# Two token chunks through one pass over the weights in the first MLP of an attention and two-MLP kernel

## The chip, the cores and the metric

One core of one Trainium2 chip runs the whole program. The metric is device time in microseconds of one execution, the median of several runs; lower is better. A profiled execution of the kernel before gives the rows that are quoted.

## The reference

Attention over 2 batches, 8 heads, 1152 keys and head size 64, with queries averaged in pairs (576 per head), then two MLPs of 1152 tokens, model width 512 and hidden width 2048. Everything is float32. The weights `w_in`, `w_out` of both MLPs reach the chip as 64-bit words, which the kernel turns into float32 itself.

```python
q_pool = q.reshape(B, H, S // factor, factor, D).mean(axis=3)
scores = scale * np.matmul(q_pool, k.transpose(0, 1, 3, 2))
attn = np.exp(scores - np.max(scores, axis=-1, keepdims=True))
attn = attn / (np.sum(attn, axis=-1, keepdims=True) + 1e-09)
x = (attn @ v)                      # then to 1152 tokens x 512
...
h = x @ w_in                        # first MLP
g = np.where(h > 0.0, h, alpha * (np.exp(np.minimum(h, 0.0)) - 1.0))
x = g @ w_out
...
h = x @ w_in                        # second MLP
sp = np.where(h > 20.0, h, np.log1p(np.exp(np.minimum(h, 20.0))))
out = (h * np.tanh(sp)) @ w_out
```

## The kernel before

**Numbers in two parts.** Each operand of a product is kept as a rounded part (`h`, written with a cast to F32R on ScalarE, ACT) and the remainder (`l`, a subtraction on VectorE, DVE, or GpSimd, POOL). A product is three matmuls: high by high, high by low, low by high. PE is TensorE, SP the engine whose queue issues all DMAs.

**Attention.** `Attention.run` (line 696) writes a list of events for 72 tiles of 128 queries: scores (`wide`, `rest`), their maxima on DVE, exponentials on ACT, turning the probabilities with PE (`pst`), splitting them into two parts on ACT, DVE and POOL, and the product with the values (`psv`). Every event has a due time in `PP['x']`, in units of tiles; the list is sorted by it, and that is the order of every engine's queue. The last events (`finish`, line 684) multiply by the reciprocal sums and write `xh` and `xl`, the tokens in two parts, 576 per batch; `xl` is line 694.

**Weights.** There are 32 tiles of weights in each MLP: 16 steps over the hidden width, each with one tile of `w_in` and one of `w_out`, 128x512. In `need` their number is j = 2 * step + (0 for `w_in`, 1 for `w_out`). A tile is converted from 64-bit words by a chain of one Abs on ACT and four operations on DVE (`Weights.chain`, lines 821 to 826, in the attention; `weight`, lines 1040 to 1051, in the MLPs), then cast and subtracted (lines 1064 and 1067; `PP['wd']` lists the tiles whose subtraction is on DVE, the others are on POOL). Five tiles are converted in the attention and stay in SBUF (`fs`, `gs`). Twelve more (`cs0` to `cs11`, `PP['ncs']`; those not in `PP['d1']`) are converted in the attention, stored to DRAM and loaded again in the MLP, since SBUF has no room for them. The tiles in `d1` are converted in the first MLP. While the first MLP runs, many tiles of the second are converted and stored too (`PP['c2']`), and each tile of the second MLP then takes the place of one of the first.

**MLPs.** Each MLP goes through three chunks of tokens (`z1`: 512, 384 and 256 columns; `z2`: three of 384), and each chunk through all 16 steps, so there are 96 steps in a row. A step s has `U{s}` (`up`, line 946: twelve matmuls into one PSUM tile), the gate `g{s}_0` and on (`gate`, line 986), `D{s}` and `E{s}` (`down`, line 958: the eight matmuls with the gate's high part, and four with the low part, summed over the 16 steps in PSUM). PSUM has eight banks: a ring of four for `up` and four for the sums. The gate of the first MLP reads and writes the PSUM tile itself: Relu and Exp on ACT, one operation on DVE (line 1001), the cast to `gh` on ACT (1025), the subtraction to `gl` on DVE (1027). At the end of a chunk `evac` writes the sums to SBUF. `PP['y']` has a due time for each of these events and each link of a weight's chain, in steps; they are sorted, and that is again the order of every queue. On PE it begins like this:

```
U0 U1 U2 U3 D0 U4 E0 D1 E1 U5 D2 E2 U6 U7 D3 U8 E3 D4 E4 D5 U9 E5 U10 D6 D7 E6 U11
```

Of the kernel before, what the change touches and what calls it, by code (L numbers as in the profile page):

```python
# [24 lines left out]
P = 128  # L25
# [18 lines left out]
    'd1': [1, 4, 7, 10, 12, 13, 15, 17, 18, 20, 21, 23, 24, 26, 27, 29, 30, 31],  # L44
    'c2': {'1': 15, '3': 13, '5': 18, '7': 19, '9': 20, '11': 25, '13': 22, '15': 21, '17': 24, '19': 24, '21': 26, '23': 27, '25': 28, '27': 29, '29': 29, '31': 31, '30': 17, '0': 30, '24': 30, '18': 7, '12': 6, '16': 11, '22': 17},
    'ng': 4,
    'wd': [1, 4, 2, 0, 42, 15, 43, 11, 26, 57, 37, 21, 56, 28, 31, 38, 47, 46, 61, 45, 60, 17, 30, 18, 22, 6],
    'upb': 4,
    'man': 'pavgs',
    'wa': [5, 7, 8, 9, 10, 11, 12, 13],  # L50
# [8 lines left out]
    'z1': [512, 384, 256],  # L59
    'z2': [384, 384, 384],  # L60
    'pool': [0, 2, 4, 5, 8, 10, 11, 14, 15, 17, 20, 22, 23],
    'ncs': 12,
# [794 lines left out]
def build(ctx, tc, q, k, v, w1_in, w1_out, w2_in, w2_out, out):  # L857
# [55 lines left out]
    with ExitStack() as actx:  # L913
# [7 lines left out]
        Attention(nc, tc, actx, q, k, v, ident, xh, xl, ps2, ps1, raw).run(aside)  # L921

    wa, wp, gp, tmp = pool("wa", 1), pool("wp", 1), pool("gp", 1), pool("mtmp", PP.get('tb', 2))
    ups, accs = pool("ups", PP['upb'], space=PSUM), pool("accs", 8 - PP['upb'], space=PSUM)
    for key in need:
        if key == PP['odd']:
            W.place[key] = [spare.pop(), wp.tile([P, DM], F32R, name="wo")]
# [225 lines left out]
```

## Time and profile before

| what | us |
|---|---|
| median of 3 runs | 683.97 |
| lowest and highest | 683.75, 684.83 |
| the profiled execution | 684.13 |
| its span, first to last instruction | 682.4 |

The profile has 11870 instructions. In its rows a line like L954 is a line of the kernel; `out<-in` are the names of tiles; a busy time is the sum over a group, and a mean is of one instruction. Matmuls overlap, so the mean of one is longer than the time from one to the next, and the ends of matmuls are modelled.

### The profile page before, as it was taken

Reading aid. Unit: us, or ns where it says so; the run is one execution under the profiler, and the core shown is the slowest. Engines: PE = TensorE matmul, PEld = TensorE weight load, DVE = VectorE, ACT = ScalarE, POOL = GpSimd, SP = SyncE. Lnnn points to the kernel's source line nnn. Section 1 sums busy time; section 2 is a strip of 40 time slices with the busy share of each in tenths; the row PEclk is TensorE's granted clock in tenths of the full one; section 3 lists DMA queues with packets and bytes.
Section 4 is the critical chain, followed back from the end, with each engine's and each line's share of the span. In section 5 each row is a group of like instructions: output and inputs, shape, how many; then the busy total and the mean of one; then the engine's idle time right before and its main releaser. Section 6 shows DMA issues by size and latency. Waiting matters only on the chain.

```text
span 682.4 us, 11870 instructions
## 1 busy us (share of the span) xinstructions
PE 666.1 (98%) x4007; PEld 602.2 (88%) x4007; DVE 586.2 (86%) x1111; ACT 480.2 (70%) x1125; POOL 266.8 (39%) x308
## 2 busy tenths in 40 slices
PE   7999999999999998999999999999999999999997
PEld 5898989888888887888888999999999999989996
DVE  5999899999898998789998887787998886977885
ACT  5999999999999999576765553576655543535453
POOL 2778787878787888352220000133230100000000
PEclk9999999999999999999999999999999999999999
DMA  7678586848675651665443676647120000101001
GB/s 218 160 180 232 134 219 161 216 103 191 184 173 147 170 161 32 197 228 182 167 140 138 214 225 194 201 125 227 51 79 1 1 0 1 48 0 47 0 1 48
DMA packets 65181, 88.64 MB, mean 130 GB/s; under 512 B 22296, under 2 KB 40544, under 8 KB 65120
## 3 DMA queue, kind: packets, MB, share of 16 engines
q1 hardware_dynamic: 65120, 87.88, 45.4%
q8 instruction: 32, 0.52, 0.3%
q14 instruction: 29, 0.24, 0.1%
HBM read 59.24 MB, written 11.57 MB: 104 GB/s over the span
## 4 chain that ended last, share of the span: by engine, by line
PE 80%; ACT 12%; DVE 3%; issue 2%; DMA 1%; POOL 1%; SPq 0%; ACTq 0%; DVEq 0%; POOLq 0%
PE up L954 29%; PE acc L984 29%; PE psv L667 7%; PE pst L627 7%; PE wide L572 5%; ACT a L596 4%; ACT whole L642 2%; ACT th L652 2%; PE rest L572 2%; ACT a L594 1%; DMA qr<-in_q_dram 1%; DVE neg L582 1%; ACT avlo L680 1%; ACT kh L485 1%; DVE tl L654 1%
## 5 line engine op out<-in xcount | busy, mean ns | idle before, releaser
L954 PE MATMUL up<-xh,wp 128*128 128x384 f32 (+2 forms) x576 | 154.0, 336 | 0.0
L434 POOL TENSOR_TENSOR tl<-whole,th 128x384 fp32r<-128x384 f32 (+1 forms) x112 | 114.1, 1019 | 9.3
L627 PE MATMUL pst<-ident,a 128*128 128x128 f32 x648 | 103.6, 277 | 7.5 <-ACT whole L642 3.4
L954 PEld LDWEIGHTS up<-xh,wp 128*128 128x128 f32 x576 | 103.6, 188 | 5.3 <-DVE gl L1027 0.4
L954 PE MATMUL up<-xl,wp 128*128 128x384 f32 (+2 forms) x288 | 96.6, 335 | 0.0
L627 PEld LDWEIGHTS pst<-ident,a 128*128 128x128 f32 x648 | 75.2, 140 | 22.4 <-ACT whole L642 8.9
L1067 POOL TENSOR_TENSOR wp<-wt,wp 128x512 fp32r<-128x512 f32 x32 | 45.7, 1441 | 120.8 <-ACT wp L1064 90.6
L667 PE MATMUL psv<-th,vs 128*128 128x320 f32 (+1 forms) x288 | 89.0, 327 | 1.4 <-ACT whole L642 1.0
L667 PE MATMUL psv<-tl,vs 128*128 128x320 f32 (+1 forms) x288 | 79.9, 295 | 0.0
L582 DVE TENSOR_REDUCE neg<-wide 128x1 f32<-128x898 f32 x72 | 78.0, 1083 | 0.4
L433 POOL TENSOR_SCALAR th<-whole 128x384 fp32r<-128x384 f32 (+1 forms) x112 | 61.8, 551 | 39.0 <-ACT whole L642 29.4
L596 ACT ACTIVATE a<-wide,neg 128x896 f32<-128x896 f32 x72 | 73.9, 1026 | 0.8 <-DVE neg L582 0.4
L654 DVE TENSOR_TENSOR tl<-pst,th 128x384 fp32r<-128x384 f32 (+1 forms) x128 | 60.4, 498 | 12.0 <-ACT th L652 11.0
L1004 ACT ACTIVATE e<-up 128x384 f32<-128x384 f32 x48 | 23.7, 494 | 59.2 <-PE up L954 40.5
L984 PE MATMUL acc<-wp,gh 128*128 128x512 f32 x252 | 64.1, 391 | 0.0
L1027 DVE TENSOR_TENSOR gl<-up,gh 128x384 fp32r<-128x384 f32 (+2 forms) x96 | 52.6, 552 | 13.2 <-ACT gh L1025 6.7
L984 PE MATMUL acc<-gh,wp 128*128 128x512 f32 (+2 forms) x336 | 63.8, 335 | 0.0
L1025 ACT CAST gh<-up 128x384 fp32r<-128x384 f32 (+2 forms) x96 | 45.0, 478 | 23.3 <-DVE up L1023 13.6
L984 PEld LDWEIGHTS acc<-gh,wp 128*128 128x128 f32 x336 | 54.8, 189 | 4.4
L652 ACT CAST th<-pst 128x384 fp32r<-128x384 f32 (+1 forms) x128 | 53.3, 455 | 7.5 <-PE pst L627 3.8
L572 PE MATMUL wide<-ks,qh 128*128 128x448 f32 (+1 forms) x160 | 57.7, 375 | 0.0
L667 PEld LDWEIGHTS psv<-th,vs 128*128 128x128 f32 x288 | 54.4, 189 | 3.6 <-ACT whole L642 1.6
(150 smaller groups left out, 1570.4 us busy)
## 6 DMA issues: line engine op xcount, KB each, us to landing
raw<-in_moe_w_out_dram SPq DMA_DIRECT2D x23, 512.0 KB, 4.8
w<-wt SPq DMA_DIRECT2D x35, 256.0 KB, 3.5
wt<-w SPq DMA_DIRECT2D x35, 256.0 KB, 3.2
raw<-in_moe_w_in_dram SPq DMA_DIRECT2D x17, 512.0 KB, 4.9
wp<-in_moe_w_in_dram SPq DMA_DIRECT2D x13, 512.0 KB, 6.9
kr<-in_k_dram SPq DMA_DIRECT2D x16, 288.0 KB, 5.3
vr<-in_v_dram SPq DMA_DIRECT2D x8, 576.0 KB, 4.0
wp<-in_moe_w_out_dram SPq DMA_DIRECT2D x9, 512.0 KB, 6.1
```

The costliest lines, as they stand in the source:

```text
L433: nc.gpsimd.tensor_scalar(hi, x, 1.0, 1.0, op0=ALU.mult, op1=ALU.mult)
L434: nc.gpsimd.tensor_tensor(lo, x, hi.bitcast(F32), op=ALU.subtract)
L572: nc.tensor.matmul(dst, w[:], x[:, cols], start=(o == 0), stop=(o == len(ops) - 1))
L582: nc.vector.tensor_reduce(neg[:], wide[:, :, :WW + 1], axis=AX.XY, op=ALU.max, negate=True)
L596: nc.scalar.activation(a[:, :2 * WW].rearrange("p (c x) -> p c x", c=2), wide[:, :, :WW], AF.Exp, bias=neg[:], accum_out=self.sums[n][:, t ...
L627: nc.tensor.transpose(ps[:, i * P:(i + 1) * P], a[:, j * P:(j + 1) * P], self.ident[:])
L652: nc.scalar.copy(h, src[:, :, x0:x0 + w])
L654: nc.vector.tensor_tensor(l, src[:, :, x0:x0 + w], h.bitcast(F32), op=ALU.subtract)
L667: nc.tensor.matmul(ps[:, :w], self.VS[n % 2][:, h, j].rearrange("p a d -> p (a d)"), t[:, j, :w], start=(c == 1), stop=(c == 2 * NKT))
L954: nc.tensor.matmul(ps, w, x, start=(o == 0), stop=(o == len(ops) - 1))
L984: nc.tensor.matmul(ps[:, :x.shape[1]], a, x, start=(i == 0 and o == 0 and not low), stop=(i == NFF - 1 and low == 1))
L1027: tt(gl, h, gh.bitcast(F32), op=ALU.subtract)
```

## The change

The first two chunks of the first MLP, 512 and 256 tokens, go through the 16 steps together. The new list of steps has three wide steps first, then alternates wide and narrow ones, and ends with three narrow ones; the third chunk (384) and the second MLP follow as before. There are 96 steps still. Each narrow step runs three pairs behind the wide step with the same weights.

Since two chunks are summed at once, PSUM is divided anew: four banks for the wide sums, two for the ring of `up` (tag `up`), and two (tag `upb`) that serve as part of the ring for the first four steps, then hold the four narrow sums, two of 256 columns in each bank, and return to the ring from step 36 on. A gate of the first MLP now begins with a copy of the PSUM tile to SBUF on ACT (`p`), which frees the tile; the four operations that follow read and write `p`.

The number of tiles stored in the attention falls from twelve to nine (`ncs`; `d1` has three more tiles). `wd` loses ten tiles of the first MLP, whose subtractions go to POOL. `wa` (which pool a weight tile's place is taken from) has other tiles. All due times in `x` and `y` are new. On PE the new order is, from the start and around step 13:

```
U0 U1 U2 U3 D0 U4 E0 D1 U5 E1 U6 D2 E2 U7 U8 D3 D4 E3 U9 D5 U10 E4 D6 D7 E5 U11 D8 E6 E7
U12 D9 D10 D11 U13 U14 E8 E9 U15 D12 E10 E11 U16 E12 D13 U17
```

```diff
-    'd1': [1, 4, 7, 10, 12, 13, 15, 17, 18, 20, 21, 23, 24, 26, 27, 29, 30, 31],
+    'd1': [1, 4, 7, 9, 10, 11, 13, 14, 15, 17, 18, 19, 21, 22, 23, 25, 26, 27, 29, 30, 31],
...
-    'wd': [1, 4, 2, 0, 42, 15, 43, 11, 26, 57, 37, 21, 56, 28, 31, 38, 47, 46, 61, 45, 60, 17, 30, 18, 22, 6],
+    'wd': [1, 4, 2, 0, 42, 43, 57, 37, 56, 38, 47, 46, 61, 45, 60, 6],
...
-    'wa': [5, 7, 8, 9, 10, 11, 12, 13],
+    'wa': [5, 7, 9, 10, 11, 13, 14, 15],
...
-    'z1': [512, 384, 256],
+    'z1': [512, 256, 384],
...
-    'ncs': 12,
+    'ncs': 9,
...
-    ups, accs = pool("ups", PP['upb'], space=PSUM), pool("accs", 8 - PP['upb'], space=PSUM)
+    ups, accs = pool("ups", 2, space=PSUM), pool("accs", 4, space=PSUM)
...
-    steps = [(m, c, i) for m in range(2) for c in range(len(Z[m])) for i in range(NFF)]
+    wide, thin = ([(0, c, i) for i in range(NFF)] for c in range(2))
+    lag = 3
+    steps = wide[:lag] + [x for p in zip(wide[lag:], thin) for x in p] + thin[-lag:]
+    steps += [(0, 2, i) for i in range(NFF)] + [(1, c, i) for c in range(3) for i in range(NFF)]
+    paired = 2 * NFF
...
-        hid[s] = ps = ups.tile([P, 512], F32, name="up")[:, :z]
+        hid[s] = ps = ups.tile([P, 512], F32, name="up" if 4 <= s < paired + 4 or s % 2 else "upb")[:, :z]
...
-            acc[m, c] = [accs.tile([P, 512], F32, name="acc") for _ in range(units)]
+            if (m, c) == (0, 1):
+                halves = [ups.tile([P, 512], F32, name="upb") for _ in range(2)]
+                acc[m, c] = [x[:, y:y + 256] for x in halves for y in (0, 256)]
+            else:
+                acc[m, c] = [accs.tile([P, 512], F32, name="acc") for _ in range(units)]
...
-            nc.tensor.matmul(ps[:, :x.shape[1]], a, x, start=(i == 0 and o == 0 and not low), stop=(i == NFF - 1 and low == 1))
+            shared = (m, c) == (0, 1)
+            nc.tensor.matmul(ps[:, :x.shape[1]], a, x, start=(i == 0 and o == 0 and not low and not (shared and u % 2)),
+                             stop=(i == NFF - 1 and low == 1), skip_group_check=shared)
...
         if m == 0:
+            p = t("p")
             if k == 0:
-                act(t("e"), h, AF.Relu, scale=-1.0)
+                nc.scalar.copy(p, h)
             if k == 1:
+                act(t("e"), p, AF.Relu, scale=-1.0)
+            if k == 2:
                 act(t("e"), t("e"), AF.Exp, scale=-1.0)
-            if k == 2:
-                stt(out=h, in0=t("e"), scalar=-1.0, in1=h, op0=ALU.add, op1=ALU.max)
+            if k == 3:
+                stt(out=p, in0=t("e"), scalar=-1.0, in1=p, op0=ALU.add, op1=ALU.max)
+            h = p
```

## Rows read from the trace of the kernel before

**Rows 1.** The page, busy us of each engine, share of the span, instructions.

```profile
PE 666.1 (98%) x4007; PEld 602.2 (88%) x4007; DVE 586.2 (86%) x1111; ACT 480.2 (70%) x1125; POOL 266.8 (39%) x308
```

**Rows 2.** By stage: stretch, length, busy us of each engine (x), PEclk, DMA share, GB/s.

```profile
0.00:20.00 20.00, 15.26 (x88) 10.37 (x89) 12.76 (x23) 12.73 (x30) 7.57 (x21) 1.00 0.79 216
20.00:260.00 240.00, 234.64 (x1653) 212.01 (x1653) 220.43 (x393) 228.93 (x591) 192.35 (x234) 1.00 0.67 170
260.00:278.60 18.60, 16.16 (x110) 13.90 (x109) 15.97 (x33) 15.87 (x39) 11.72 (x16) 1.00 0.10 30
278.60:356.20 77.60, 77.60 (x343) 63.66 (x342) 72.16 (x124) 51.16 (x93) 25.05 (x17) 1.00 0.60 201
356.20:411.00 54.80, 54.80 (x303) 52.98 (x302) 46.03 (x90) 31.10 (x63) 1.30 (x1) 1.00 0.57 183
411.00:460.00 49.00, 49.00 (x355) 49.00 (x354) 37.43 (x78) 27.59 (x67) 8.55 (x7) 1.00 0.58 178
```

**Rows 3.** The page, the chain that ended last, share of the span by engine.

```profile
PE 80%; ACT 12%; DVE 3%; issue 2%; DMA 1%; POOL 1%; SPq 0%; ACTq 0%; DVEq 0%; POOLq 0%
```

**Rows 4.** Shapes on ACT, 20 to 260 us: count, busy, mean ns, idle before.

```profile
L821 ACT ACTIVATE wt<-raw 128x512 f32<-128x512 f32 x12 | 8.3, 691 | 0.0
```

**Rows 5.** Shapes on DVE, 20 to 260 us.

```profile
L826 DVE SCALAR_TENSOR_TENSOR wt<-raw,wt 128x512 int32<-128x512 int32 x12 | 9.9, 824 | 0.0
L824 DVE SCALAR_TENSOR_TENSOR wt<-raw,wt 128x512 int32<-128x512 int32 x13 | 9.5, 728 | 0.0
L823 DVE TENSOR_SCALAR wt<-wt 128x512 int32<-128x512 int32 x13 | 9.1, 698 | 0.0
...
L822 DVE TENSOR_SCALAR wt<-wt 128x512 f32<-128x512 f32 x13 | 6.8, 520 | 0.2
```

**Rows 6.** Timeline of PE, 278.5 to 292 us: start, us, what.

```profile
278.62 0.39 PE L954 MATMUL up<-xh,wf 128*128 128x512 f32 x1
...
289.57 1.98 PE L984 MATMUL acc<-gh,vr 128*128 128x512 f32 x8
```

**Rows 7.** Timeline of PE, 425 to 437 us, a narrow up.

```profile
432.98 0.28 PE L954 MATMUL up<-xh,kr 128*128 128x256 f32 x1
...
434.41 0.86 PE L984 MATMUL acc<-gl,wp 128*128 128x384 f32 x4
```

**Rows 8.** Timeline of ACT, 264 to 292 us, the cast of gate 0.

```profile
286.77 0.58 ACT L1025 CAST gh<-up 128x512 fp32r<-128x512 f32 x1
```

**Rows 9.** Timeline of DVE, 283 to 293 us.

```profile
286.40 1.13 DVE L694 TENSOR_TENSOR xl<-xf,xh 128x576 fp32r<-128x576 f32 x1 [2.02 <-ACT xh L692]
...
288.66 1.64 DVE L1049 SCALAR_TENSOR_TENSOR wt<-wp,wt 128x512 int32<-128x512 int32 x1
```

**Rows 10.** Shapes on ACT, 278.6 to 356.2 us and 411 to 460 us.

```profile
L997 ACT ACTIVATE e<-up 128x512 f32<-128x512 f32 x16 | 9.4, 594 | 2.7 <-PE up L954 2.7
...
L997 ACT ACTIVATE e<-up 128x256 f32<-128x256 f32 x12 | 4.6, 386 | 2.6 <-PE up L954 1.5 <-DVE up L1001 0.7 <-ACT wt L1040 0.4
```

**Rows 11.** Shapes on DVE, 278.6 to 356.2 us.

```profile
L1049 DVE SCALAR_TENSOR_TENSOR wt<-wp,wt 128x512 int32<-128x512 int32 x15 | 13.9, 926 | 0.1
L1051 DVE SCALAR_TENSOR_TENSOR wt<-wp,wt 128x512 int32<-128x512 int32 x15 | 12.9, 859 | 0.2
...
L1001 DVE SCALAR_TENSOR_TENSOR up<-e,up 128x512 f32<-128x512 f32 x14 | 9.4, 686 | 0.1
...
L1067 DVE TENSOR_TENSOR wp<-wt,wp 128x512 fp32r<-128x512 f32 x9 | 6.1, 683 | 0.0
...
L1049 DVE SCALAR_TENSOR_TENSOR wt<-raw,wt 128x512 int32<-128x512 int32 x4 | 2.7, 679 | 0.0
```

**Rows 12.** Waits of ACT, 278.6 to 411 us: total, times, longest us.

```profile
ACT wp L1064 <- DVE wt L1051: 9.1, 6, 2.5
...
ACT wt L1040 <- DVE wt L1049: 4.9, 1, 4.9
```

**Rows 13.** Timeline of POOL, 284 to 300 us.

```profile
288.46 1.29 POOL L1067 TENSOR_TENSOR wo<-wt,qr 128x512 fp32r<-128x512 f32 x1 [1.53 <-ACT qr L1064]
```

More of the change, by code (lines that the diff above doesn't have):

```diff
@@ L992, in t @@
             if (s, x) not in tmps:
-                tmps[s, x] = tmp.tile([P, ZM if x == "e" else max(PP['z2'])], F32, name=x)[:, :h.shape[1]]
+                tmps[s, x] = tmp.tile([P, max(PP['z2']) if x == "n" else ZM], F32, name=x)[:, :h.shape[1]]
             return tmps[s, x]
         if m == 0:
+            p = t("p")
             if k == 0:
-                act(t("e"), h, AF.Relu, scale=-1.0)
+                nc.scalar.copy(p, h)
             if k == 1:
+                act(t("e"), p, AF.Relu, scale=-1.0)
+            if k == 2:
                 act(t("e"), t("e"), AF.Exp, scale=-1.0)
-            if k == 2:
-                stt(out=h, in0=t("e"), scalar=-1.0, in1=h, op0=ALU.add, op1=ALU.max)
+            if k == 3:
+                stt(out=p, in0=t("e"), scalar=-1.0, in1=p, op0=ALU.add, op1=ALU.max)
+            h = p
         else:
@@ L1023, in gate @@
                 stt(out=h, in0=t("p"), scalar=-1.0, in1=h, op0=ALU.mult, op1=ALU.mult)
-        if k == (9 if m else 3):
+        if k == (9 if m else 4):
             nc.scalar.copy(gh, h)
-        if k == (10 if m else 4):
+        if k == (10 if m else 5):
             tt(gl, h, gh.bitcast(F32), op=ALU.subtract)
@@ L1096, in build @@
         add(f'E{s}', down, s, 1)
-        for k in range(11 if m else 5):
+        for k in range(11 if m else 6):
             add(f'g{s}_{k}', gate, s, k)
```

522 rows, old and new, of the table PP are left out of this document.

## The prediction

> **What bounds it now.** I read the page's busy shares first, then a table by stage, then the chain's shares, then the shapes and timelines of the two stages that the change touches. PE is busy 98% of the span [rows 1], so the first guess is that no time is left. The table corrects that in two ways [rows 2]. From 278.6 to 460 us, the first MLP, PE's busy time equals the length of every stretch at full granted clock: 77.60 of 77.60, 54.80 of 54.80, 49.00 of 49.00. Nothing that another engine does faster there can shorten it; it can only be lengthened. From 20 to 260 us, the attention, three engines are nearly full at once: PE 234.64 of 240 us, ACT 228.93 (95.4%), DVE 220.43 (91.8%). PE's figure there is soft, since matmul ends are modelled. Of the chain ACT holds 12% and DVE 3% [rows 3], and with PE full in the MLP these shares belong almost wholly to the attention. So the attention is paced by ACT and PE handing work to each other, with DVE close behind, and it is the one place where removed work can pay.
>
> **The change part by part.** *Nine tiles stored, not twelve.* For each of the three chains removed from the attention ACT does one Abs of 0.691 us [rows 4] and DVE four operations of 0.520, 0.698, 0.728 and 0.824 us, together 2.77 us [rows 5]. Three chains are 2.07 us of ACT and 8.31 us of DVE; three loads and three stores leave SP's queue too, where nothing on the chain waits behind them. What the span gains lies between two ends. Weighted by the chain, ACT's 12% and DVE's 3% of 682.4 us are 82 and 20 us; held against the 278.6 us up to the MLP that is 29% and 7%, so 0.6 + 0.6 = 1.2 us. If DVE's whole relief reached the end it would be 8.3 us. If ACT keeps its idle share, its 2.07 us alone are 2.07 / 0.954 = 2.2 us. I take ACT's 2.2 us, ACT being the fullest engine after PE, and add DVE's chain-weighted 0.6: a gain of 2.8 us.
>
> *Orders anew in the attention.* Nothing else is added or removed there; which instruction stands ahead of which changes throughout. The trace cannot price this. Its room is PE's idle time at both ends: 4.74 us in the first 20 us and 2.44 us from 260 to 278.6 [rows 2]. I take 0 and keep 2 us either way.
>
> *The first steps of the MLP.* The old order has U0 to U3 (10.95 us of matmuls) ahead of D0 [rows 6], and so has the new one. Gate 0's cast ended at 286.77 + 0.58, 2.2 us before D0 [rows 8]; the added copy takes 0.59 us of that, and 1.6 us stay. The new U4 is the first narrow step and reads tokens 512 to 767, whose last part, xl of the last pair, ended at 287.53 [rows 9], 4 us before D0's end at 291.55, behind which U4 stands. Cost 0; with that cover gone, each microsecond of lateness is a microsecond of span.
>
> *One pass for two chunks.* The matmuls are the same in number and width (512, 256 and 384 columns in place of 512, 384 and 256), so PE's own work stays. Twelve take 2.74 us at 512 columns (10.95 / 4) [rows 6] and 1.43 at 256 (434.41 less 432.98) [rows 7]. A pair of steps is 24 matmuls of each width, 5.5 + 2.9 = 8.3 us for two weight tiles, where the old first chunk left 5.5. Weights are due later, but PE did not wait for them: gain 0.
>
> *Copies to SBUF.* ACT gets 48. The nearest rows are its first reads of the same PSUM tiles: 0.594 us at 512 columns and 0.386 at 256 [rows 10], halfway 0.49 at 384; 16 times 1.47 is 23.5 us. ACT is idle for 26.4 + 23.7 + 21.4 = 71.5 us between 278.6 and 460 [rows 2], which hides them.
>
> *Work brought into the MLP.* Three more chains, again 8.3 us of DVE and 2.1 of ACT at most. Ten subtractions of the first MLP go from DVE (0.683 us) [rows 11] to POOL (1.29) [rows 13]: DVE loses 6.8 us, POOL gains 13. DVE, idle for 25.8 us from 278.6 to 460, ends about where it was, and POOL is nearly idle after 356 [rows 2]. Three full loads replace three reloads; the DMA share was 0.60 at most. Cost 0, but see the rivals.
>
> *Ring of first products.* Four PSUM tiles become two while the narrow chunk's sums hold the other two banks. Adding up the new order with the step times above, the time from the end of a U to the U that reuses its tile is mostly 5 to 8 us, in seven cases under 5, the least 2.8 (U13 to U15: U14, E8 and E9 lie between). A copy of 0.59 us fits if ACT is not more than 2.2 us late; its single waits for conversions were 2.5 us long, once 4.9 [rows 12]. Bounds: 0, or seven cases of about 0.7 us, 5 us. I take 0, the nearest row being a PE without any wait in this stage.
>
> **Sum.** The profiled execution's 684.13 us (span 682.4 and 1.7 around it) less 2.8 is 681.3. It lies 0.16 us over the median of 683.97; I forecast medians: 683.97 - 2.8 = 681.2 us.
>
> **The rivals.** *The port (slower).* The copy gives both DVE operations of a first-MLP gate two SBUF inputs where they had one. Such an operation stretches when it meets POOL: the conversion at 288.66 took 1.64 us [rows 9] beside a POOL subtraction from 288.46 to 289.75 [rows 13]. From 278.6 to 356.2 the conversions took 0.926 and 0.859 us on some tiles and 0.679 on others, while the gates, with one input in PSUM, took 0.686 [rows 11]. Worked out from these: about 0.2 us for each of 64 gate operations in the paired pass, 13 us, on a DVE that was busy for 118.2 of the 132.4 us from 278.6 to 411 [rows 2]. With 8.3 us of chains, and less 3.4 us for half of the subtractions, DVE would need 136 us in 132. It decides from the point at which a gate ends later than its D is due; with half of the 13 us, 6.5, reaching PE the time is 681.2 + 6.5 = 687.7 us. Against it: in the first 77.6 us DVE was 93% busy already, and PE did not wait. Chance 0.13. The Trainium skill, SBUF — State Buffer, section "Who interferes with whom", has a rule for this: a VectorE instruction with two SBUF inputs and a GpSimd instruction that reads SBUF exclude each other for a whole instruction. By that rule, with which the 1.64 us agree, the price above is the change's own.
>
> *The ring (slower).* Copies stand in ACT's queue behind its waits for loads and conversions: 681.2 + 5 = 686.2 us, chance 0.07. *Nothing arrives.* The freed time in the attention is taken up by another wait, because PE, ACT and DVE hand the chain around: the chain-weighted 1.2 us or less, 682.8 us or a little over; chance 0.18. *DVE is the true pace.* Then 8.3 us go: 675.7 us. For it: DVE at 92%, with operations stretched there as well (0.824 us, where 0.679 is the undisturbed time); against it, DVE's small part of the chain. Chance 0.10. That the chains are not removed can be excluded: the lists say which tiles are converted early.
>
> **How the numbers follow.** The forecast, chance 0.52, spans 679 to 682.6. A measurement of this kernel can tell about 0.2% (1.4 us) from no change, so faster means below 682.6: 0.52 + 0.10 = 0.62. Same is the third rival, 0.18. Slower is the port and the ring, 0.20. The range runs from 676.5, most of the way to the DVE rival, to 687.5, close to the port's price; about a tenth lies beyond each end.
>
> **What would show it.** Right: the first up matmul starts near 275.8 instead of 278.62; three Abs fewer in the attention (12 stood from 20 to 260 us); ACT still above 95% there and DVE near 90%; PE busy for the whole of every MLP stretch; 48 copies of about 0.59, 0.49 and 0.39 us on ACT. The port: gate operations of more than 0.75 us at 512 columns, and PE idle ahead of acc matmuls, released by DVE or ACT. The ring: PE idle ahead of up matmuls, released by ACT's copy. I am wrong in the main step if the first up matmul does not move, or if PE loses more than 1 us between it and 660 us.

## The result, and the profile after

The changed kernel takes 690.45 us (median of 4 runs, 690.09 to 691.96) where the kernel before took 684.40 beside it (683.75 to 685.22). The ratio is 1.010, interval 1.0088 to 1.0111: slower, by 6.05 us. 681.2 us and faster had been forecast; the range ended at 687.5.

Two numbers split the result. The first up matmul starts at 274.60 us in place of 278.62 [rows 6], so the attention is 4.0 us shorter. From there to the end of the span it takes 690.2 - 274.6 = 415.6 us, before 682.4 - 278.6 = 403.8: the MLPs are 11.8 us longer. The profiled execution took 691.96 us, 1.5 over the median, so that these two numbers add up to 7.8 and not to 6.05; what is read from the profile below belongs to that execution.

The page of the changed kernel: the span, the busy line, and the chain that ended last.

```profile
span 690.2 us, 11927 instructions
...
PE 666.9 (97%) x4007; PEld 605.1 (88%) x4007; DVE 591.8 (86%) x1101; ACT 501.0 (73%) x1173; POOL 289.6 (42%) x318
...
PE 71%; ACT 9%; issue 6%; DVE 5%; DMA 5%; POOL 3%; SPq 0%; POOLq 0%; ACTq 0%; DVEq 0%
```

The busy line hardly differs from [rows 1]; the chain does [rows 3]: PE falls from 80% to 71%, POOL rises from 1% to 3%, and DMA and "issue" now hold 11%. A chain that leaves PE says that something else set PE's time. The table by stage says where (stretch, length, busy us of PE, PEld, DVE, ACT, POOL, then PEclk, DMA share, GB/s):

```profile
20.00:260.00 240.00, 234.48 (x1673) 216.61 (x1672) 217.44 (x388) 229.46 (x598) 190.52 (x237) 1.00 0.64 161
260.00:275.00 15.00, 13.39 (x94) 12.13 (x94) 12.48 (x26) 12.74 (x31) 10.28 (x13) 1.00 0.05 9
275.00:300.00 25.00, 23.41 (x112) 19.02 (x112) 18.02 (x28) 17.98 (x35) 10.85 (x7) 1.00 0.78 271
300.00:320.00 20.00, 20.00 (x110) 17.41 (x109) 19.26 (x37) 15.60 (x34) 6.76 (x4) 1.00 0.47 159
320.00:340.00 20.00, 17.46 (x93) 14.96 (x92) 15.20 (x27) 10.30 (x21) 10.25 (x4) 0.91 0.58 184
340.00:360.00 20.00, 18.23 (x102) 15.25 (x100) 18.22 (x31) 12.08 (x25) 8.23 (x5) 1.00 0.54 174
360.00:380.00 20.00, 18.03 (x99) 15.02 (x100) 17.77 (x33) 14.52 (x29) 7.55 (x4) 1.00 0.77 260
380.00:400.00 20.00, 20.00 (x114) 17.56 (x113) 18.89 (x38) 13.18 (x28) 5.12 (x3) 1.00 0.32 100
400.00:440.00 40.00, 40.00 (x261) 38.94 (x260) 36.93 (x70) 30.55 (x68) 6.51 (x4) 1.00 0.71 227
```

Before, PE's busy time equalled the length of every stretch of the first MLP [rows 2]. Now it falls short by 1.6 us in 275 to 300, 2.5 in 320 to 340, 1.8 and 2.0 in the two stretches behind: in all 7.9 us, every one inside the paired pass. From 400 us on PE is full again, up to an idle end like that of before. The other 4 us of the 11.8 stand in PE's busy time, 404.2 us from the first up to the end where it was 400.1: the granted clock is 0.91 in 320 to 340, so that PE is slower there while it works (some 1.5 us, worked out below). What makes up the rest no row tells. Note DVE: it is busy for 103.88 of the 120 us from 280 to 400, less than the 108.11 of before. A busier DVE is not what PE waits for.

PE's waits from 274.6 to 402 us, total, times and longest in us:

```profile
PE acc L997 <- ACT gh L1043: 2.9, 3, 1.1
PE acc L997 <- POOL wp L1085: 2.5, 1, 2.5
PE up L962 <- ACT p L1012: 2.4, 3, 0.9
```

The single longest is 2.5 us behind a subtraction on POOL. The other two name ACT: its cast of the gate, and its copy. But ACT waits itself. Its own waits over the same stretch:

```profile
ACT p L1012 <- DVE gl L1045: 13.8, 10, 3.7
ACT gh L1043 <- DVE p L1018: 5.7, 9, 1.7
...
ACT wt L1058 <- POOL wp L1085: 4.9, 5, 1.7
```

ACT's copy waits ten times, 13.8 us, for one of the two buffers of `p`, which gl, the last DVE operation of an earlier gate, gives back; its cast waits nine times for the DVE operation before it. So these waits go back to DVE's gates, and ACT's waits for POOL's subtractions come on top. The chain of waits around the longest stop, and POOL's timeline there (start, us, what):

```profile
319.94 3.58 POOL wp L1085 x2
323.51 2.95 issue
...
326.50 5.33 POOL wp L1085
```

```profile
326.50 6.74 POOL L1085 TENSOR_TENSOR wp<-wt,wp 128x512 fp32r<-128x512 f32 x2 [2.99 <-ACT wp L1082]
```

One subtraction of 128x512 took 5.33 us. Before, one that began ahead of its DVE neighbour took 1.29 [rows 13], and it was the neighbour that stretched [rows 9]. DVE's timeline over the same microseconds says what it did meanwhile:

```profile
326.26 0.68 DVE L1067 SCALAR_TENSOR_TENSOR wt<-raw,wt 128x512 int32<-128x512 int32 x1
326.87 0.41 DVE L1065 TENSOR_SCALAR wt<-wt 128x512 int32<-128x512 int32 x1
327.20 0.68 DVE L1018 SCALAR_TENSOR_TENSOR p<-e,p 128x512 f32<-128x512 f32 x1
...
330.28 0.41 DVE L1065 TENSOR_SCALAR wt<-wt 128x512 int32<-128x512 int32 x1
331.61 0.50 DVE L1018 SCALAR_TENSOR_TENSOR p<-e,p 128x256 f32<-128x256 f32 x1 [0.91 <-ACT e L1016]
332.03 1.76 DVE L1045 TENSOR_TENSOR gl<-p,gh 128x512 fp32r<-128x512 f32 x1
```

From 326.26 to 330.69 DVE issues nine operations back to back, each at its undisturbed length (0.68 or 0.41 us). Then it idles for 0.91 us, and POOL's subtraction ends at 331.83, 1.14 us after DVE's last: about the time that it takes undisturbed. So it seems to have stood still behind nearly the whole row. The last line is the same lock the other way round: POOL's next subtraction begins at 331.83, and DVE's gl at 332.03 takes 1.76 us. The Trainium skill, SBUF — State Buffer, section "Who interferes with whom", states that such a lock is held for an instruction and that the order of issue decides who is blocked; these lines agree, and go further: one POOL instruction lost to a row of DVE's.

What the stop then costs PE, in its timeline:

```profile
328.94 0.39 PE L997 MATMUL acc<-gh,wp 128*128 128x512 f32 x1
331.88 3.25 PE L997 MATMUL acc<-gh,wp 128*128 128x512 f32 x7 [2.54 <-POOL wp L1085]
334.93 0.63 PE L962 MATMUL up<-xh,wp 128*128 128x512 f32 x1
```

The seven matmuls take (334.93 - 331.88) / 7 = 0.44 us each, about twice the 0.23 us of a full row [rows 6: twelve in 2.74]. That is the lower of the two clock levels, 1.2 GHz, behind a PE that stood idle (the granted clock is 0.57 from 331.5 to 335 us); it adds some 1.5 us to the 2.5. Last, the shapes from 274.6 to 402 us (count, busy, mean ns, idle before), first DVE's, then POOL's:

```profile
L1063 DVE TENSOR_SCALAR wt<-wt 128x512 f32<-128x512 f32 x34 | 18.8, 561 | 9.4 <-ACT wt L1058 9.4
...
L1067 DVE SCALAR_TENSOR_TENSOR wt<-wp,wt 128x512 int32<-128x512 int32 x19 | 14.8, 789 | 0.0
L1045 DVE TENSOR_TENSOR gl<-p,gh 128x512 fp32r<-128x512 f32 x14 | 12.8, 918 | 1.4 <-ACT gh L1043 1.2
...
L1018 DVE SCALAR_TENSOR_TENSOR p<-e,p 128x512 f32<-128x512 f32 x15 | 11.5, 767 | 1.8 <-ACT e L1016 1.8
```

```profile
L1085 POOL TENSOR_TENSOR wp<-wt,wp 128x512 fp32r<-128x512 f32 x25 | 47.7, 1919 | 73.1 <-ACT wp L1082 51.9 <-DMA raw<-in_moe_w_out_dram 11.6 <-DVE wt L1063 5.4
```

Gates grew from 0.686 [rows 11] to 0.918 and 0.767 us; POOL's 25 subtractions average 1.919 us. POOL is busy for less than half of the stretch and still late: its share says nothing, its single delays do.

### The profile page after: what moved, and what is told of

Same layout as the page of the kernel before. It is cut to its first block, busy times and chain, and to the rows that moved or that the text cites. A ratio compares the mean times of both kernels' runs of the same rounds, so it can differ in the third digit from the quotient of the medians.

```text
span 690.2 us, 11927 instructions
## 1 busy us (share of the span) xinstructions
PE 666.9 (97%) x4007; PEld 605.1 (88%) x4007; DVE 591.8 (86%) x1101; ACT 501.0 (73%) x1173; POOL 289.6 (42%) x318
## 4 chain that ended last, share of the span: by engine, by line
PE 71%; ACT 9%; issue 6%; DVE 5%; DMA 5%; POOL 3%; SPq 0%; POOLq 0%; ACTq 0%; DVEq 0%
PE acc L997 21%; PE up L962 13%; PE upb L962 9%; PE psv L671 9%; PE pst L631 8%; PE wide L576 6%; POOL wp L1085 3%; ACT a L600 2%; PE rest L576 2%; PE upb L997 2%; ACT th L656 2%; DMA raw<-in_moe_w_out_dram 1%; ACT whole L646 1%; DMA wp<-in_moe_w_out_dram 1%; DMA qr<-in_q_dram 1%
## 5 line engine op out<-in xcount | busy, mean ns | idle before, releaser
L1085 POOL TENSOR_TENSOR wp<-wt,wp 128x512 fp32r<-128x512 f32 x42 | 71.3, 1712 | 146.8 <-ACT wp L1082 118.1
L962 PE MATMUL up<-xh,wp 128*128 128x384 f32 (+2 forms) x384 | 104.2, 338 | 1.8 <-ACT p L1012 1.8
L962 PEld LDWEIGHTS up<-xh,wp 128*128 128x128 f32 x384 | 69.0, 189 | 8.1 <-ACT p L1012 3.3
L658 DVE TENSOR_TENSOR tl<-pst,th 128x384 fp32r<-128x384 f32 (+1 forms) x128 | 60.6, 499 | 13.6 <-ACT th L656 12.4
L962 PE MATMUL up<-xl,wp 128*128 128x384 f32 (+2 forms) x192 | 64.6, 336 | 0.0
L576 PE MATMUL wide<-ks,qh 128*128 128x448 f32 (+1 forms) x160 | 61.4, 398 | 0.1
L997 PE MATMUL acc<-gh,wp 128*128 128x512 f32 (+1 forms) x224 | 51.0, 372 | 4.4 <-POOL wp L1085 2.5
L997 PEld LDWEIGHTS acc<-wp,gh 128*128 128x128 f32 x252 | 47.1, 188 | 9.2
L671 PEld LDWEIGHTS psv<-tl,vs 128*128 128x128 f32 x288 | 54.7, 190 | 0.0
L646 ACT COPY whole<-pst 128x384 f32<-128x384 f32 x104 | 51.8, 498 | 2.0 <-PE pst L631 1.2
L962 PE MATMUL upb<-xh,wp 128*128 128x384 f32 x192 | 52.8, 335 | 0.0
```

What stands on the lines that cost most here:

```text
L576: nc.tensor.matmul(dst, w[:], x[:, cols], start=(o == 0), stop=(o == len(ops) - 1))
L658: nc.vector.tensor_tensor(l, src[:, :, x0:x0 + w], h.bitcast(F32), op=ALU.subtract)
L671: nc.tensor.matmul(ps[:, :w], self.VS[n % 2][:, h, j].rearrange("p a d -> p (a d)"), t[:, j, :w], start=(c == 1), stop=(c == 2 * NKT))
L962: nc.tensor.matmul(ps, w, x, start=(o == 0), stop=(o == len(ops) - 1))
L997: nc.tensor.matmul(ps[:, :x.shape[1]], a, x, start=(i == 0 and o == 0 and not low and not (shared and u % 2)), stop=(i == NFF - 1 and low ...
L1085: e.tensor_tensor(l[:], t[:], h[:].bitcast(F32), op=ALU.subtract)
```

## The experiments

The theory after reading this: *the copies give DVE's gates two SBUF inputs, ten more subtractions stand on POOL, the two engines hold each other up, and PE stops behind late weight tiles and gates.* Its rivals: the ring of two PSUM tiles; the three conversion chains brought into the MLP; too much work on one engine, whatever it reads; and, which no run was made for, the two buffers of `p`. Thirteen kernels were run, in four groups, each beside runs of the kernel before (medians 683.79, 684.04, 683.70 and 683.93 us). Ratios are to those. "First up" and PE's busy time in the 120 us from 280 to 400 come from each kernel's one profile. In five profiles with the attention of the kernel before, its own with them, first up lies from 278.30 to 279.16; in seven with the new one from 273.77 to 275.32. So one profile places it to about 1 us. Where kernels of two groups are compared in us, it is by their differences to the runs of the kernel before in their own group (the change: +6.05).

| kernel | median us | ratio, interval | first up | PE busy of 120 |
|---|---|---|---|---|
| before | 683.97 | | 278.62 | 120.00 |
| after | 690.45 | 1.010, 1.0088 to 1.0111 | 274.60 | 112.13 |
| wd_back | 696.68 | 1.019, 1.0164 to 1.0216 | 275.32 | 108.93 |
| ncs12 | 691.53 | 1.0122, 1.0100 to 1.0143 | 275.26 | 112.45 |
| wd_alone | 690.81 | 1.0103, 1.0088 to 1.0118 | 278.37 | 114.65 |
| copy_alone | 698.14 | 1.0215, 1.0198 to 1.0232 | 278.30 | 112.66 |
| x_alone | 681.56 | 0.9961, 0.9946 to 0.9976 | 274.43 | 119.12 (274.4 to 394.4) |
| copy_dummy | 686.00 | 1.0027, 1.0017 to 1.0036 | 278.70 | 118.83 |
| pool_zero | 680.45 | 0.9942, 0.9925 to 0.9960 | 275.24 | 119.94 |
| ring4 | 704.58 | 1.0293, 1.0253 to 1.0333 | 274.39 | 112.20 |
| pool_zero3 | 681.23 | 0.9954, 0.9936 to 0.9972 | 273.80 | 119.02 |
| pool_ten | 684.24 | 1.0008, 0.9996 to 1.0020 | 273.77 | 116.95 |
| no_pool | 691.05 | 1.0099, 1.0080 to 1.0118 | 275.08 | 111.13 |
| chains_out | 683.71 | 0.9995, 0.9986 to 1.0004 | 277.84 | 120.00 |
| copy_zero3 | 689.46 | 1.0077, 1.0060 to 1.0094 | 279.16 | 118.80 |

### One part undone, one part alone

**wd_back**: the changed kernel with the ten subtractions back on DVE.

```diff
-    'wd': [1, 4, 2, 0, 42, 43, 57, 37, 56, 38, 47, 46, 61, 45, 60, 6],
+    'wd': [1, 4, 2, 0, 42, 15, 43, 11, 26, 57, 37, 21, 56, 28, 31, 38, 47, 46, 61, 45, 60, 17, 30, 18, 22, 6],
```

> The changed kernel (690.45 us, 6.05 over the kernel before) with one part undone: the ten subtractions of first-MLP weights that it moved to POOL are on DVE again. Starved subtraction (POOL's subtractions are held up by DVE's operations with two SBUF inputs, and PE waits for them, at worst 2.5 us with 5.33 us for one subtraction): PE waits for POOL go, the clock stays up, PE loses under 3 us in the MLP, 683 to 685.5 us. Ring of two (copies late in ACT's queue): the waits of up for the copy stay, 2.4 us and more, 687 to 689 us. DVE load (three chains too many in the MLP): 6.8 us more on DVE, 690 to 693 us.

696.68 us, 12.9 over the kernel before and 6.8 over the change, above all three expectations. PE's waits, 280 to 402 us:

```profile
PE up L962 <- DVE wp L1085: 3.8, 1, 3.8
PE acc L997 <- DVE wp L1085: 3.5, 2, 3.3
```

The waits went with the subtractions: PE now waits for the same tiles on DVE, where they stand in a longer queue, while the 17 that stayed on POOL still average 2.1 us. So moving them back is no cure; the due times were made for them on POOL, and the run doesn't tell how much of its loss comes from that.

**wd_alone**: the same line, the other way round, in the kernel before.

> The kernel before with one part of the change alone: the ten subtractions go from DVE to POOL. Starved subtraction as an effect of the gates' second SBUF input: the old gates leave POOL its reads, a subtraction lasts about 1.5 us on average from 278 to 356 us, and the time stays at 684 to 685.5 us. If the move to POOL alone is the fault: PE waits for POOL and 687 to 690 us. DVE load: 683 to 684.5 us, DVE having 6.8 us less.

690.81 us: 7.0 slower with nothing else changed. POOL's subtractions are not longer than in the kernel before (mean 1.46 us, there 1.48), but there are ten more in its queue and PE waits for them (280 to 402 us):

```profile
PE acc L984 <- POOL wp L1067: 3.2, 2, 2.3
PE up L954 <- DVE gl L1027: 1.2, 1, 1.2
```

So the moved subtractions have a price of their own, with the old pass and without copies.

**copy_alone**: the kernel before with the copy, for the 44 steps of its first MLP up to s = 43.

```diff
...
+            p = t("pn"[s % 2]) if s < 44 else h
...
+                if s < 44:
+                    nc.scalar.copy(p, h)
+                act(t("e"), p, AF.Relu, scale=-1.0)
...
+                stt(out=p, in0=t("e"), scalar=-1.0, in1=p, op0=ALU.add, op1=ALU.max)
+            h = p
```

> The kernel before with the copy to SBUF alone, for the first 44 of the 48 first-MLP steps (steps and ring of four unchanged; the tiles of the copies have four buffers under two names). Starved subtraction: POOL's subtractions lengthen from 1.495 us on average (278 to 356 us) to 1.8 or more, gate operations on DVE from 0.686 to 0.75 or more, and PE loses 1 to 5 us: 685 to 689 us. Ring of two: with four tiles a copy does no harm, 683.5 to 685 us.

698.14 us: 14.3 slower, where at most 5 had been expected, with a ring of four PSUM tiles and all tiles and subtractions where they were. Of shapes from 278.3 to 356 us, DVE's gates and POOL's subtractions:

```profile
L1031 DVE TENSOR_TENSOR gl<-p,gh 128x512 fp32r<-128x512 f32 x6 | 7.1, 1176 | 2.6 <-ACT gh L1029 2.6
L1004 DVE SCALAR_TENSOR_TENSOR p<-e,p 128x512 f32<-128x512 f32 x6 | 6.3, 1052 | 0.0
```

```profile
L1071 POOL TENSOR_TENSOR wp<-wt,wp 128x512 fp32r<-128x512 f32 x13 | 23.4, 1813 | 39.7 <-ACT wp L1068 39.7
```

Both sides of the lock are longer: gates 1.18 and 1.05 us on half of the buffers (0.686 before [rows 11]; on the other half, `n`, 0.90 and 0.68), subtractions 1.81, the longest 4.84. PE's largest waits from 280 to 402 us are for both:

```profile
PE acc L984 <- ACT gh L1029: 2.5, 2, 1.5
PE up L954 <- POOL wp L1071: 1.7, 2, 1.1
```

In that stretch no copy waits for a buffer that gl gives back (one does behind it, 2.5 us), so the buffers of the copies are not what this run pays for there. In the change, where they are two, pool_zero below still waits 9.4 us for them and loses nothing on PE.

**ncs12**: the changed kernel with twelve stored tiles, so that the three chains are done in the attention again.

```diff
-    'd1': [1, 4, 7, 9, 10, 11, 13, 14, 15, 17, 18, 19, 21, 22, 23, 25, 26, 27, 29, 30, 31],
+    'd1': [1, 4, 7, 10, 13, 15, 17, 18, 19, 21, 22, 23, 25, 26, 27, 29, 30, 31],
-    'ncs': 9,
+    'ncs': 12,
-    Y = PP['y']
+    Y = dict(PP['y'])
+    for j in (9, 11, 14):
+        Y[f'w{j}_d'] = Y[f'w{j}_h'] - 1.5
```

> The changed kernel with twelve tiles stored in the attention, as before the change (tiles 9, 11 and 14 go back; their loads in the MLP are due 1.5 steps ahead of the cast). DVE load: the MLP's stalls go mostly, the attention is 3 to 4 us longer again: 684 to 687 us. Starved subtraction: most stalls stay, since the ten subtractions are still on POOL: 690 to 694 us. Ring of two: likewise, 691 to 694 us. For all: the first up matmul starts at 277.5 to 279 us instead of 274.6.

691.53 us, +7.7, and PE busy for 112.45 of 120: no better than the change. The three chains brought into the MLP are not its fault. First up came at 275.26, where every rival had put it at 277.5 or later: taking the chains out of the attention moved it by 0.7 us, less than the spread.

### What part of the copy costs

**copy_dummy**: copy_alone with the copies made and never read; the gates stay on PSUM.

```diff
...
+            p = h
...
+                if s < 44:
+                    nc.scalar.copy(t("pn"[s % 2]), h)
...
```

> The kernel before with the same 44 copies on ACT as in the run copy_alone, but nobody reads them: the gates work on PSUM as before. Port (gates with two SBUF inputs and POOL exclude each other): POOL's subtractions are back at about 1.47 us, 684 to 688 us, against 698.14 with the copies in use. ACT load or the longer gate: 694 to 698 us.

686.00 us. ACT's work alone costs 2.0 us of the 14.3; the other 12.4 come with reading the copy from SBUF. POOL's subtractions over the same 278.3 to 356 us:

```profile
L1071 POOL TENSOR_TENSOR wp<-wt,wp 128x512 fp32r<-128x512 f32 x15 | 21.8, 1462 | 43.2 <-ACT wp L1068 43.2
```

They are back at 1.46 us (1.50 in the kernel before, same stretch), and the gates at 0.689 and 0.683. One operand's memory makes the difference.

**copy_zero3**: copy_alone, with each POOL subtraction of the first MLP replaced by three memsets of the same tile, which write SBUF and read nothing.

```diff
-                e.tensor_tensor(l[:], t[:], h[:].bitcast(F32), op=ALU.subtract)
+                if e is nc.gpsimd and key[0] == 0:
+                    for _ in range(3):
+                        e.memset(l[:].bitcast(F32), 0.0)
+                else:
+                    e.tensor_tensor(l[:], t[:], h[:].bitcast(F32), op=ALU.subtract)
```

> As copy_alone (698.14 us), with each of POOL's subtractions of a first-MLP weight in the MLP replaced by three memsets of 1.7 us together, which read nothing in SBUF. Port: the loss of copy_alone goes, as with the unread copies (686.0 us): 684 to 688 us, gate operations on DVE at 0.64 us on average. If the copy's place in the gate (data through SBUF, not the meeting with POOL) is the fault: 694 to 699 us.

689.46 us, +5.5, above the 684 to 688 expected for the port: 8.8 of the 14.3 us go with these reads of POOL. In 280 to 400 PE is busy for 118.80, as with the unread copies (118.83). Of the 3.6 us that stay above copy_dummy, 2.6 are PE's idle time from 440 to 520 us, where it is busy for 77.43 of 80. There POOL works on weights of the second MLP, which this run left as subtractions that read, beside the last gates with copies (256 columns wide), while the very last four gates stand on PSUM. DVE, 425 to 520 us:

```profile
L1031 DVE TENSOR_TENSOR gl<-n,gh 128x256 fp32r<-128x256 f32 x6 | 5.4, 926 | 0.7 <-ACT gh L1029 0.7
...
L1031 DVE TENSOR_TENSOR gl<-up,gh 128x256 fp32r<-128x256 f32 x4 | 1.7, 422 | 1.9 <-ACT gh L1029 1.9
```

So the same stretching stands where reads of POOL were left; no run takes these away too.

### The ring

**ring4**: the changed kernel with four PSUM tiles for the first products throughout; the narrow chunk's sums are added on top of the wide chunk's, in the same banks.

```diff
-        hid[s] = ps = ups.tile([P, 512], F32, name="up" if 4 <= s < paired + 4 or s % 2 else "upb")[:, :z]
+        hid[s] = ps = ups.tile([P, 512], F32, name="up" if s % 2 else "upb")[:, :z]
...
-                halves = [ups.tile([P, 512], F32, name="upb") for _ in range(2)]
-                acc[m, c] = [x[:, y:y + 256] for x in halves for y in (0, 256)]
+                acc[m, c] = [x[:, :256] for x in acc[0, 0]]
...
```

> The changed kernel with a ring of four first products throughout: the narrow chunk's sums go on top of the wide ones in the same four banks (both chunks' results are wrong sums; the number and width of matmuls stay). Ring of two: no wait of up for the copy, PE loses 4 to 6 us less, 684 to 687 us. Port: the wait for POOL and those of acc for the gates stay, 688 to 691 us.

704.58 us, but not for the reason that would speak for the ring. In 280 to 400 PE is busy for 112.20, as in the change (112.13), and its waits there are (280 to 402 us):

```profile
PE acc L996 <- ACT gh L1042: 4.6, 4, 2.8
PE acc L996 <- POOL wp L1084: 3.1, 2, 2.8
```

No up waits for a copy any more, and the same time is lost at the acc matmuls. So the ring of two was the place where the lateness showed, not its source; pool_zero below, which has the same ring, says so without this run's own faults. The further loss is the experiment's own: PE is busy for 31.18 of the 40 us behind 400, where the shared banks have to be emptied.

### POOL's reads

**pool_zero**: the changed kernel with POOL's subtractions of the first MLP replaced by one memset each.

```diff
-                e.tensor_tensor(l[:], t[:], h[:].bitcast(F32), op=ALU.subtract)
+                if e is nc.gpsimd and key[0] == 0:
+                    e.memset(l[:].bitcast(F32), 0.0)
+                else:
+                    e.tensor_tensor(l[:], t[:], h[:].bitcast(F32), op=ALU.subtract)
```

> The changed kernel; every subtraction of a first-MLP weight in the MLP that stands on POOL is a memset to zero instead, so POOL reads nothing there (the low parts of these weights are left out of the result). Port: waits for POOL go and the gates on DVE are short again, PE loses under 3 us in the MLP, 681 to 684 us. Ring of two: waits of up for the copy stay, 686 to 689 us.

680.45 us, -3.6, so 9.6 below the change, and PE is busy for 119.94 of 120. DVE's shapes, 274 to 402 us, and POOL's:

```profile
L1063 DVE TENSOR_SCALAR wt<-wt 128x512 f32<-128x512 f32 x37 | 16.3, 444 | 8.7 <-ACT wt L1058 8.6
...
L1067 DVE SCALAR_TENSOR_TENSOR wt<-wp,wt 128x512 int32<-128x512 int32 x19 | 12.8, 684 | 0.0
...
L1045 DVE TENSOR_TENSOR gl<-p,gh 128x512 fp32r<-128x512 f32 x16 | 11.0, 688 | 1.7 <-ACT gh L1043 1.0 <-ACT wp L1082 0.3
L1018 DVE SCALAR_TENSOR_TENSOR p<-e,p 128x512 f32<-128x512 f32 x16 | 11.0, 685 | 3.0 <-ACT e L1016 2.9
```

```profile
L1086 POOL MEMSET wp<- 128x512 f32 x25 | 14.1, 580 | 93.2 <-DVE wt L1069 45.9 <-ACT gh L1043 18.7 <-ACT e L1016 13.3
```

Every stretched shape falls back: gates from 0.918 and 0.767 to 0.688 and 0.685, conversions from 0.789 to 0.684. The copies, the ring of two, the paired order and the three chains are all still there. This is no usable kernel (it leaves out part of the weights' lower halves), but it gives almost the whole loss back: from the first up to the first up of the third chunk (384 columns) it takes 403.86 - 275.24 = 128.6 us, the change 414.37 - 274.60 = 139.8, and from there to the end of the span both take 275.8.

It also makes POOL's work shorter, so **pool_zero3** gives it three memsets per subtraction, as in copy_zero3: some 1.7 us each.

> As pool_zero (680.45 us), but each subtraction of a first-MLP weight on POOL is replaced by three memsets of the same tile, about 3 x 0.58 = 1.7 us, longer than an undisturbed subtraction of 1.3 us and still without a read of SBUF. Port (the shared reads are the fault): 680 to 682.5 us, no loss on PE over 1 us. Latency (POOL simply ends later than DVE would): waits for POOL come back, 685 to 690 us.

681.23 us, -2.5, an interval that overlaps pool_zero's. POOL is busy for 46.67 of the 120 us, as in the change (47.00), and PE for 119.02. With POOL as busy as in the change and reading nothing, 8.5 of the 9.6 us are still back: the length of POOL's work alone is not the matter.

Besides not reading, a memset differs in one more thing: it needn't wait for ACT's cast of its tile. The 27 low parts that POOL makes in the first MLP were done on average 0.15 us behind the end of their tile's cast in pool_zero3, and 2.68 us behind it in the change. So the runs with memsets take a wait away together with the reads, and how they share the 8.5 us isn't shown. The lengths of DVE's operations are free of that, and so is the pair copy_alone and copy_dummy, where POOL makes the same subtractions behind the same casts.

**pool_ten**: only the ten moved subtractions become a memset; the old ones stay.

```diff
+                if key[0] == 0 and 2 * key[2] + key[1] in (15, 11, 26, 21, 28, 31, 17, 30, 18, 22):
+                    e.memset(l[:].bitcast(F32), 0.0)
...
```

> The changed kernel with memsets to zero in place of only the ten subtractions that the change moved to POOL; the other sixteen stay subtractions. If the move of the ten is the whole fault: 681 to 683 us. If the second SBUF input of the gates starves every subtraction: POOL's remaining subtractions still last 1.8 us and more on average, PE loses 3 to 6 us, 684 to 687 us.

684.24 us, +0.5: with these ten alone 5.5 of the 9.6 us are back, with the others too 4.1 more. The subtractions that stayed still average 1.85 us (274 to 402 us), the wide gates 0.755 and 0.832, and PE loses 3.05 of the 120 us: the move of the ten is not the whole fault.

**no_pool**: all subtractions of the first MLP on DVE, so that POOL reads nothing there and the computation is whole (`wd` lists 0 to 31 and the eleven others).

> The changed kernel with all subtractions of the first MLP on DVE, none on POOL. DVE gains 26 x 0.684 = 17.8 us in the paired pass and loses its stretching, about 10 us. Port: conversions and gates are back at 0.68 us and no operation lasts over 1 us, but the queue of DVE is fuller and out of its order: 684 to 690 us. DVE load or order: over 690 us, PE waiting for DVE's subtractions.

691.05 us, +7.4, no better than the change. DVE's operations are undisturbed (0.68 us each), but PE waits for the queue (280 to 402 us):

```profile
PE up L962 <- DVE wp L1085: 4.7, 2, 3.4
PE acc L997 <- ACT gh L1043: 1.7, 2, 1.1
PE acc L997 <- DVE wp L1085: 1.5, 1, 1.5
```

So in the paired pass the subtractions are late on either engine: on POOL because DVE locks it out, on DVE because they stand behind everything else.

### The attention

**x_alone**: the kernel before with the new table of due times `x` for the attention, and nothing else; twelve stored tiles, four PSUM tiles, no copies.

```diff
-        'W': -1.0749, 'R': -1.1123, 'm': -0.4683, 'M': 0.0983, 'e': 0.7836, 'E': 0.5109, 'T0': 0.7631, 'T1': 0.851, 'T2': 1.1649, 'H0': 1.1324,
+        'W': -1.1224, 'R': -1.1151, 'm': -0.5029, 'M': 0.1244, 'e': 0.857, 'E': 0.3166, 'T0': 0.734, 'T1': 0.842, 'T2': 1.1704, 'H0': 1.0942,
...
```

> The kernel before with the new due times of the attention alone (twelve tiles stored, the MLP untouched). If the attention's 4.0 us came from its new order: the first up matmul at 275 to 276 us instead of 278.62, no PE loss in the MLP, 680 to 681.5 us. If they came from the three chains: first up near 278, 683 to 684.5 us.

681.56 us, 0.9961 of the kernel before (0.9946 to 0.9976), faster than both the kernel before and the change. The first up in PE's timeline:

```profile
274.43 0.40 PE L950 MATMUL up<-xh,wf 128*128 128x512 f32 x1
```

That is 4.2 us ahead of 278.62 [rows 6], with all twelve chains still done: the order alone gives the attention's gain. Some 1 us of it is lost again behind (PE is busy for 119.12 of the 120 us from its first up).

**chains_out**: the opposite. In the kernel before, the conversion of tiles 22, 25 and 28 is left out of the attention (one memset on DVE in its place), in the old order.

```diff
+            if store and key[0] == 0 and 2 * key[2] + key[1] in (22, 25, 28):
+                return [lambda: nc.vector.memset(t[:], 0.0)] + [lambda: None] * 4
```

> The kernel before with the conversion of three of the twelve stored tiles (numbers 22, 25 and 28) left out of the attention and a memset on DVE in its place, so these weights are zero; loads, stores and orders stay. ACT loses 2.07 us and DVE about 7 us in the attention. If removed work pays as forecast: first up matmul 2 to 3 us earlier than 278.62, 681 to 682.5 us. If only the order pays: first up within 0.8 us of 278.62, 683.3 to 684.5 us.

683.71 us, 0.9995 (0.9986 to 1.0004): no difference. First up comes at 277.84, 0.8 us earlier, about the spread. Three chains are gone from the attention, for three memsets; ahead of the first up DVE is busy for 4.2 us less and ACT for 1.6, and next to nothing arrives.

## Why the prediction was wrong, and where it was right

*Nine tiles stored: a gain of 2.8 us.* The size looked nearly right (first up moved by 4.0, forecast 2.8), and for the wrong reason. Three Abs did go, from 16 to 13 ahead of the first up, but chains_out puts their worth at 0.8 us of first up and at none of the time that can be told. That lies below the chain-weighted end, 1.2, which was the third rival, "nothing arrives". So the rule of the sum, that the fullest engine's relief reaches the span by its own share, failed here; why the freed time is lost no run shows.

*Orders anew: 0, 2 us either way.* Failed, in the attention. x_alone shows 4.2 us of first up and 2.5 us of time from the order alone. The room named for it, PE's idle time of 4.74 and 2.44 us at the two ends [rows 2], holds only part of it: in x_alone it is 3.41 and 1.5 us, in the change 4.75 and 1.6. Ahead of the first up PE idles for 10.5 us in x_alone and 11.9 in the change, where it idled for 12.5; the rest is shorter busy time for the same matmuls, on the PE figure that the prediction itself called soft.

*Copies to SBUF, 0, and work brought into the MLP, 0.* The failed main step, worth 11.8 us in the profiled execution, where PE loses 7.9 us and 1 was the limit set for being right. The copies were priced as ACT's work against ACT's idle time, and that part holds nearly: copy_dummy puts it at 2.0 us. What they do to the reads of DVE was left to a rival at 0.13. The ten subtractions were priced by sums of busy time ("POOL is nearly idle after 356") at 1.29 us each, where they took 1.9 and each of them is a weight tile with a due time; wd_alone puts the move at 7.0 us in the old pass, pool_ten the ten at 5.5 in the new one.

*The port, 687.7 us.* The right mechanism, half the price, and one victim overlooked. Its signs came: wide gates over 0.75 us, and PE idle ahead of acc behind ACT's casts (2.9 us). The rival had 13 us on DVE, 0.2 on each of 64 gate operations, half reaching PE. Measured in the change: 0.23 us on 14 wide gl, 0.08 on 15 wide p, and 0.11 on 12 narrow p (0.530 against 0.419 in pool_zero), together 5.8 us; and DVE is busy for less than before. POOL's subtractions grew by more: against the 1.48 us of the kernel before in the same stage 25 x (1.92 - 1.48) = 11 us, and PE's longest single stop is behind the worst of them, 5.33. Of PE's idle time, though, 5.3 us stand behind ACT's casts and copies, which wait for DVE's gates, and 2.5 behind POOL. "Against it: in the first 77.6 us DVE was 93% busy already, and PE did not wait" was the reason for 0.13, and it does not hold: those gates had one input in PSUM, and a DVE just as busy left POOL's subtractions at 1.48 us, as copy_dummy's do (1.46, against 1.81 in copy_alone). The price had also left out the clock, which falls to 0.91 in 320 to 340, where PE stood idle.

*The ring, bounds 0 to 5, taken 0.* Right. The waits named for it are there (2.4 us of up behind ACT's copy), but ring4 removes them and loses as much elsewhere, and pool_zero keeps the ring and loses nothing. *First steps of the MLP* and *one pass for two chunks* cost nothing that shows: with POOL's reads gone PE is busy for 119.94 of 120 in the same pass.

*The sum.* The parts don't add: copy_alone and wd_alone cost 14.3 and 7.0 us in the old pass, x_alone gains 2.5, and the change comes to +6.05. Either the paired pass gives a good part back (its weights are due later, 8.3 us for two tiles where the old had 5.5), or the two losses overlap, since PE can wait for a gate and a weight at once. That is open: a paired pass whose gates stay on PSUM wasn't tried.

## What to carry to other kernels

Before an operand is moved from PSUM to SBUF, list what GpSimd reads in the same stretch: here the copy cost 2 us as work and 12 by being read, and one of the engines that suffered was one that the edit didn't touch. Price work put on a nearly idle engine by when each piece is due and by its worst case, not by that engine's free time. Where several engines are 90% full and hand work to each other, the order can hold more than removed work does, and an order that comes with a larger change is worth running by itself.

## What the runs showed of the hardware

- A POOL subtraction of 128x512 lasted 5.33 us, four times its 1.29, behind nine DVE operations issued back to back; it ended 1.14 us after the row did.
- POOL's memsets (POOL busy for 46.67 of 120 us) left DVE's operations with two inputs alone (gates 0.683 and 0.680 us in pool_zero3, 0.688 and 0.685 in pool_zero), but stretched those with one: L1063 took 0.545 us against 0.444, about as much as beside the change's subtractions (0.561). The Trainium skill, SBUF — State Buffer, section "Who interferes with whom", states both: a GpSimd operation that only writes is no matter to the second input, but is to a tensor_scalar in a mode that uses both ports; these rows agree with the first, and with the second if L1063 runs in such a mode, which no row says.
- After 2.5 us of idle PE, seven matmuls ran at 0.44 us each instead of 0.23, at a granted clock of 0.57.
